# Clustered attention and two feed-forward layers on one core: a hand-placed order re-placed, with the first two pairs prepared in another order

## The chip, the cores and the metric

One core of a Trainium2 chip runs the whole program. The metric is device time in microseconds, median of three runs; the kernel before takes 791.06 us (790.3 to 793.32).

## The reference, cut to what matters

```python
def _attn_ref(q, k, v, centroids):            # q, k, v: 2 x 8 x 768 x 64, centroids: 8 x 16 x 64
    scale = 1.0 / np.sqrt(D)
    ...
    q_assign = np.argmax(np.einsum('bhsd,hcd->bhsc', q_n, c_n), axis=-1)
    k_assign = np.argmax(np.einsum('bhsd,hcd->bhsc', k_n, c_n), axis=-1)
    mask = q_assign[:, :, :, None] == k_assign[:, :, None, :]
    scores = np.where(mask, scale * q @ k.T, -1e9)
    attn = softmax(scores)
    return attn @ v

h = relu(x @ w_in) ** 2;      y = h @ w_out       # first layer, 1536 tokens, 512 -> 2048 -> 512
h = y @ w2_in;                out = (h * cos(h)) @ w2_out   # second layer
```

## The kernel before, in words

The 16 heads are worked two at a time, as eight **pairs**. For a pair, q and k are loaded (`load_raw`), turned on TensorE (`transpose_in`, L243), copied out by ScalarE in full (`full_copy`, L259), rounded to a high part (`high_part`, L252 and L254) and reduced to a low part (`low_part`, L265, on VectorE from PSUM). Products with the centroids (`sims`, L294), a transpose (`by_token`, L312), a maximum (`largest`, L319), its spreading and turning back (`spread`, `at_max`, L335), a comparison and a small product (`one_hot`, L348; `keep_one_hot`, L355) give one-hot rows of the nearest centroid. DMAs on SyncE's queue (SP) and ScalarE's put low parts, high parts and one-hot rows side by side (`stage`, `stage_own`, `stage_oh`), so that one product gives scores with the mask in it.

Each pair is 12 **units** of work of two kinds. `s_max` (L379; **M** below) computes scores with queries on partitions, and VectorE takes the row maxima (`s_largest`, L389). Six M give the maxima of half a pair's queries: `max_parts`, `max_cast` (L404), `max_rows` (L413), `max_keep` (L420) and the DMA `stage_max` (L427) bring them back as rows of the operand of the second kind. `scores` (L446; **S** below) computes scores with keys on partitions, ScalarE takes the exponential (L456), GpSimd adds the exponentials up (`add_up`, L468), and `pv` (L476) multiplies them with v. Then come the sums of a half pair (`sums`, L491), their inverse by way of DRAM, the division, and high and low parts of the output (`combine_low`, L555, on GpSimd). M, S, transposes and `max_rows` share three PSUM units; a unit is free again when VectorE or ScalarE has read it.

What sets the order is a table of numbers: every step has a time in units, `at(when, f, ...)` collects them, and they are emitted sorted by that time; each engine then runs its own instructions in that order, and SP its DMAs. Before the table comes a stretch written out by hand (L577 to L661) that prepares pair 0 and part of pair 1. `warm` issues small products of no use (L560): 20 at the start, and five times 8 between the first M (L1025).

Weights are loaded and split into two fp32r parts by VectorE in six operations per half chunk (L142 to L138), from the second half of pair 0 on. After attention `moe` runs 96 steps, each a product into the hidden layer (L697) and one out of it (L750) two steps later; `hooks` place the end of attention between the first of them. The last half pair's sums stand in step 1, ahead of the product of step 2.

```python
        if g + LEAD < NU:
            at(g + SMAX[c], s_max, g + LEAD)
            at(g + LARGEST[c], s_largest, g + LEAD)
    for when, _, f, a in sorted(steps_, key=lambda step: step[:2]):
        f(*a)
        1: [
            *(lambda u_=u_: pv(u_) for u_ in range(NU - GROUP, NU)), lambda: move_out(last + 1), lambda: sums(last + 1),
        ],
```

Of the kernel before, what the change touches and what calls it, by code (L numbers as in the profile page):

```python
# [25 lines left out]
LEAD = 9  # L26
# [4 lines left out]
WARM = 20  # L31
WARM_STEP = 8

FA = 8


@with_exitstack
def tile_kernel(ctx: ExitStack, tc: tile.TileContext, q, k, v, centroids, w1i, w1o, w2i, w2o, out):
# [177 lines left out]
    def load_heads(t, src, n, e=nc.sync):  # L216
        b, hp = pairs[n]
        e.dma_start(t, src[b, 2 * hp : 2 * hp + 2].rearrange("j (p t) d -> p t j d", t=NT))

    def load_raw(n, names, e=nc.sync):  # L220
        for nm in names:
            if nm == "v":
                t = ap.tile([P, NT, 2, D], F32, tag="rawv", name=f"rawv{n}", bufs=2)
            else:
                t = prepp.tile([P, NT, 2, D], F32, tag=f"raw{nm}", name=f"raw{nm}{n}")
            load_heads(t, {"q": q, "k": k, "v": v}[nm], n, e)
            raw[n, nm] = t
# [334 lines left out]

    cb = prepp.tile([P, NP, GC], F32, name="cb")
# [4 lines left out]
    load_raw(0, "q")  # L568
    load_raw(0, "k", nc.scalar)
    nc.scalar.activation(eps, half_t, AF.Exp)  # L570
    nc.gpsimd.memset(cb, 0.0)
    nc.vector.tensor_tensor(c2, cw, cw, ALU.mult)
# [3 lines left out]

    def constants(e, i):  # L577
        for j in range(2):
            e.memset(xq[i][R * (j + 1) : R * (j + 2)].bitcast(F32), 0.0)
            e.memset(xk[i][R * (j + 1) : R * (j + 2)].bitcast(F32), 0.0)  # L580

    def constants_own(e, i):
        for t in sets[i][:3]:
            for rows in OUTER:
                e.memset(t[rows, S:].bitcast(F32), -1.0 / R)

    def selection():
# [13 lines left out]
        nc.scalar.copy(first_of[:, : 2 * GC], firstf[:, : 2 * GC])  # L601
        nc.scalar.activation(first_of[:, 2 * GC :], firstf[:, 2 * GC :], AF.Copy, scale=-1.0)
# [6 lines left out]
        return first_of, oh_above, oh_scale  # L609
# [15 lines left out]
    transpose_in(0, "q")  # L625
    transpose_in(0, "k")
    full_copy(0, "q")
    full_copy(0, "k")
    load_raw(1, "qk")
    constants(nc.gpsimd, 0)  # L630
    first_of, oh_above, oh_scale = selection()
    constants_own(nc.gpsimd, 0)
    constants(nc.gpsimd, 1)
    for i in range(1, 3):
        constants_own(nc.gpsimd, i)
    high_part(0, "q", nc.vector)
    high_part(0, "k", nc.vector)
    stage(0, "k")
    stage_own(0)
    sims(0)  # L640
    keep_sims(0)
    by_token(0)
    largest(0)
    spread(0)
    low_part(0, "q")
    stage(0, "q")
    transpose_in(1, "q")
    at_max(0)
    compare(0)
    full_copy(1, "q")  # L650
    high_part(1, "q")
    one_hot(0)
    keep_one_hot(0)
    stage_oh(0, nc.scalar)
    low_part(0, "k")
    low_part(1, "q")
    transpose_in(1, "k")
    full_copy(1, "k")
    high_part(1, "k")
    low_part(1, "k")  # L660
    load_raw(0, "v")  # L661
# [196 lines left out]
    def moe(hooks):  # L858
# [38 lines left out]

    prep = [
        (-24.355, load_raw, "k"),
        (-22.864, load_raw, "q"),  # L900
        (-18.958, transpose_in, "k"),
        (-18.745, high_part, "k"),
        (-18.693, transpose_in, "q"),
        (-18.435, high_part, "q"),
        (-18.433, full_copy, "k"),
        (-18.030, low_part, "k"),
        (-17.583, full_copy, "q"),
        (-17.581, low_part, "q"),
        (-15.947, sims),
        (-15.367, keep_sims),  # L910
        (-13.090, by_token),
        (-12.080, largest),
        (-11.338, spread),
        (-9.239, at_max),
        (-9.222, compare),
        (-7.670, stage_own),
        (-7.153, one_hot),
        (-7.110, stage, "q"),
        (-6.620, keep_one_hot),
        (-4.098, stage, "k"),  # L920
        (-3.604, stage_oh),
    ]
    prep_second = [
        (-166.809, sims),
        (-141.396, keep_sims),
        (-140.871, by_token),
        (-123.691, largest),
        (-102.665, stage, "k"),
        (-94.621, spread),
        (-90.950, at_max),  # L930
        (-72.434, stage_own),
        (-39.797, stage, "q"),
        (-26.064, compare),
        (-10.377, one_hot),
        (-7.158, keep_one_hot),
        (-4.251, stage_oh),
    ]
    prep_all = [(4.558, load_raw, "v")]

    maxima = [  # L940
        (1.939, max_parts),
        (3.001, max_cast),
        (4.187, max_rows),
        (4.366, max_keep),
        (4.828, stage_max),
# [3 lines left out]
        (6.829, sums),  # L949
        (7.247, move_sums),  # L950
        (7.757, deal_sums),
        (9.940, invert),
        (9.986, move_out),
        (12.600, store_inverse),
        (13.702, load_inverse),
        (15.756, divide),
        (16.507, combine_high),
        (18.203, combine_low),
# [138 lines left out]
```

## Time and profile before

| | |
|---|---|
| median of three runs | 791.06 us |
| the profiled execution: its own time | 790.41 us |
| its span, first to last instruction | 788.4 us |
| TensorE (PE) busy | 765.1 us, 97% |
| VectorE (DVE) busy | 584.5 us, 74% |
| ScalarE (ACT) busy | 358.9 us, 46% |
| GpSimd (POOL) busy | 239.2 us, 30% |
| granted TensorE clock, mean | 0.994 |

Attention fills the first 262.8 us, the feed-forward layers the rest. A busy TensorE in this profile can still be one whose matmuls start late, since the ends are modelled; what a stage loses is read from its waits and from starts. Times in rows are microseconds from the start of the span.

### The profile page before, as it was taken

How to read it: one execution, taken by the hardware profiler on the slowest of the kernel's cores; microseconds unless marked ns; L12 is line 12 of the kernel's file. 1: busy time of each engine (PE TensorE's matmuls, PEld its weight loads, DVE VectorE, ACT ScalarE, POOL GpSimd, SP SyncE). 2: the span in 40 equal slices, each digit the busy share in tenths (PEclk: the TensorE clock that was granted, in tenths of full speed). 3: DMA queues.
4: the chain of work that ended last, by engine and by line, in shares of the span. 5: the costliest groups of instructions: out<-in, count | busy, mean ns of one | idle time of the engine just before them, and what ended most of it. 6: DMA issues, size and time to landing. Idle time of an engine off the chain costs nothing.

```text
span 788.4 us, 11444 instructions
## 1 busy us (share of the span) xinstructions
PE 765.1 (97%) x4293; PEld 586.1 (74%) x4293; DVE 584.5 (74%) x922; ACT 358.9 (46%) x609; POOL 239.2 (30%) x255
## 2 busy tenths in 40 slices
PE   6799999999999899999999999999999999999997
PEld 3575666666665688888888888888877788888886
DVE  4667787686789999969885216869999766676664
ACT  3265664665464445544444435353434433333332
POOL 7077797797999631000000000002222000000000
PEclk9899999999999999999999999999999999999999
DMA  4434545352335091037400005641000100010001
GB/s 121 121 94 117 135 102 137 79 122 57 110 95 186 7 373 58 0 107 242 158 29 1 0 1 166 206 128 35 0 1 1 54 1 1 0 54 1 0 1 54
DMA packets 76194, 62.19 MB, mean 79 GB/s; under 512 B 44896, under 2 KB 67436, under 8 KB 76140
## 3 DMA queue, kind: packets, MB, share of 16 engines
q1 hardware_dynamic: 74492, 60.99, 25.9%
q8 instruction: 33, 0.54, 0.3%
q10 hardware_dynamic: 1648, 0.49, 0.3%
q14 instruction: 21, 0.17, 0.1%
HBM read 48.27 MB, written 5.29 MB: 68 GB/s over the span
## 4 chain that ended last, share of the span: by engine, by line
PE 75%; DVE 16%; issue 3%; ACT 3%; POOL 1%; DMA 1%; ACTq 0%; SPq 0%; DVEq 0%; POOLq 0%
PE bank L750 27%; PE bank L697 13%; PE o_ps L697 13%; PE unit L446 7%; PE o_ps L476 5%; PE unit L379 4%; DVE ews L719 3%; DVE m L389 2%; DVE ews L718 2%; POOL acc L468 1%; DVE ews L730 1%; PE o_ps L294 1%; DVE aux L143 1%; DVE w L138 1%; DVE set L265 1%
## 5 line engine op out<-in xcount | busy, mean ns | idle before, releaser
L468 POOL TENSOR_TENSOR acc<-acc,p 128x384 f32<-128x384 f32 x128 | 139.9, 1128 | 2.8 <-ACT p L456 2.8
L750 PE MATMUL bank<-w,ewr 128*128 128x512 f32 x576 | 139.8, 391 | 0.4 <-DVE ewr L735 0.4
L750 PE MATMUL bank<-ewr,w 128*128 128x512 f32 x576 | 138.4, 389 | 0.0
L697 PE MATMUL bank<-xh,w 128*128 128x512 f32 x392 | 130.3, 394 | 0.0
L750 PEld LDWEIGHTS bank<-w,ewr 128*128 128x128 f32 x576 | 107.4, 188 | 25.4 <-POOL ewr L735 2.6
L750 PEld LDWEIGHTS bank<-ewr,w 128*128 128x128 f32 x576 | 108.1, 188 | 22.5
L735 POOL TENSOR_TENSOR ewr<-ews,ewr 128x512 fp32r<-128x512 f32 x24 | 32.8, 1365 | 302.9 <-ACT ewr L731 289.6
L389 DVE TENSOR_REDUCE m<-unit 128x2 f32<-128x768 f32 x96 | 88.8, 946 | 46.9 <-PE unit L379 42.0
L697 PE MATMUL o_ps<-xh,w 128*128 128x512 f32 x376 | 123.4, 389 | 0.0
L735 DVE TENSOR_TENSOR ewr<-ews,ewr 128x512 fp32r<-128x512 f32 x72 | 49.6, 689 | 54.9 <-ACT ewr L714 50.2
L697 PEld LDWEIGHTS bank<-xh,w 128*128 128x128 f32 x392 | 74.3, 190 | 17.1 <-issue 0.9
L697 PEld LDWEIGHTS o_ps<-xh,w 128*128 128x128 f32 x376 | 70.6, 188 | 14.7
L722 ACT ACTIVATE ews<-ews,narrow_t 128x512 f32<-128x512 f32 x48 | 34.9, 726 | 100.3 <-DVE ews L721 100.3
L456 ACT ACTIVATE p<-unit 128x768 f32<-128x768 f32 x96 | 71.0, 816 | 15.0 <-PE unit L446 13.2
L697 PE MATMUL bank<-xl,w 128*128 128x512 f32 x196 | 76.8, 392 | 0.0
L697 PE MATMUL o_ps<-xl,w 128*128 128x512 f32 x188 | 73.1, 389 | 0.0
L476 PE MATMUL o_ps<-p,rawv 128*64 128x384 f32 x384 | 69.0, 495 | 0.6 <-ACT x L527 0.6
L446 PE MATMUL unit<-set,set 64*128 64x384 f32 x512 | 65.1, 347 | 3.2 <-DVE set L265 2.0
L446 PEld LDWEIGHTS unit<-set,set 64*128 64x128 f32 x512 | 43.3, 184 | 15.3 <-issue 3.5
L137 ACT CAST w<-top 128x512 fp32r<-128x512 f32 x64 | 39.3, 616 | 32.1 <-DVE top L145 32.1
L138 DVE SCALAR_TENSOR_TENSOR w<-aux,aux 128x512 fp32r<-128x512 f32 x64 | 51.4, 803 | 1.7
L716 DVE TENSOR_SCALAR ews<-ews 128x512 f32<-128x512 f32 x48 | 20.3, 423 | 43.2 <-ACT ews L726 43.1
(122 smaller groups left out, 1074.8 us busy)
## 6 DMA issues: line engine op xcount, KB each, us to landing
wraw<-in_moe_w_in_dram SPq DMA_DIRECT2D x32, 512.0 KB
wraw<-in_moe_w_out_dram SPq DMA_DIRECT2D x32, 512.0 KB
rawq<-in_q_dram SPq DMA_DIRECT2D x8, 384.0 KB
ext<-set SPq DMA_DIRECT2D x32, 96.0 KB
rawv<-in_v_dram SPq DMA_DIRECT2D x8, 384.0 KB
rb<-row SPq DMA_DIRECT2D x32, 96.0 KB
rawk<-in_k_dram SPq DMA_DIRECT2D x7, 384.0 KB
held<-kept SPq DMA_DIRECT2D x8, 256.0 KB
```

Source lines behind the costliest of these rows:

```text
L137: nc.scalar.copy(w[:, 0], top.bitcast(F32))
L138: ve.scalar_tensor_tensor(w[:, 1], restf, 2.0**-20, power.bitcast(F32), ALU.mult, ALU.mult)
L379: nc.tensor.matmul(u[:, j, :HALF], lhsT=a[r, qs], rhs=b[r, ks], start=(p == 0), stop=(p == 1))
L389: nc.vector.tensor_reduce(d["m"][:, i, :, kh], u[:, :, :HALF], AX, ALU.max)
L446: nc.tensor.matmul(u[:, j, :HALF], lhsT=a[r], rhs=b[r, qs], start=(p == 0), stop=(p == len(ops) - 1))
L456: nc.scalar.activation(t, u[:, :, :HALF], AF.Exp, scale=SCALE)
L468: nc.gpsimd.tensor_tensor(accs[hb][:, j], a[:, j], ptiles[u_][:, j], ALU.add)
L476: nc.tensor.matmul(o_ps[0][j * D : (j + 1) * D, :HALF], lhsT=raw[n, "v"][:, kt, j, :], rhs=t[:, j], start=(kt == 0), stop=(kt == NT - 1),)
L697: nc.tensor.matmul(ph, lhsT=w[:, a, :], rhs=x[blk][:, a, :], start=(a == i == 0), stop=(a == KD - 1 and i == 2))
L722: nc.scalar.activation(e2, e2, AF.Sin, bias=hpi)
L735: e.tensor_tensor(al, e2, ah.bitcast(F32), ALU.subtract)
L750: nc.tensor.matmul(y, lhsT=a, rhs=b, start=(idx in opens and i == 0), stop=(idx in closes and i == 2))
```

## The change

Six edits. The hand-written stretch becomes a table (`prelude`) with the steps of pairs 0 and 1 in another order; pair 2 has a table of its own (`prep_third`), and so have the first 16 M (`SMAX_FIRST`). The low parts of pairs 0 to 2 are computed by GpSimd from the full copy in SBUF, not by VectorE from PSUM, and the PSUM unit is given back when the high part and the full copy are done. The first q and k are loaded head by head on two queues. The small products between the first M go, and there are 26 at the start for 20. All numbers of the steady tables are new; SHIFT is gone. The last half pair's sums stand one step later.

```diff
-WARM = 20
+WARM = 26
+FEW = 3
...
+        for j, e in enumerate(es or ()):
+            e.dma_start(t[:, :, j], src[b, 2 * hp + j].rearrange("(p t) d -> p t d", t=NT))
...
+        if n < FEW:
+            done_with(d, "t" + x)
...
-        nc.vector.tensor_tensor(
-            halves(d["l" + x]), wide(d["t" + x]), halves(d["h" + x].bitcast(F32)), ALU.subtract
-        )
+        high = d["h" + x].bitcast(F32)
+        if n < FEW:
+            nc.gpsimd.tensor_tensor(d["l" + x], d["f" + x], high, ALU.subtract)
+            return
+        nc.vector.tensor_tensor(halves(d["l" + x]), wide(d["t" + x]), halves(high), ALU.subtract)
...
-    load_raw(0, "q")
-    load_raw(0, "k", nc.scalar)
+    load_raw(0, "qk", (nc.sync, nc.scalar))
...
+    constants_own(nc.vector, 2)
+    for i in range(2):
         constants_own(nc.gpsimd, i)
...
+    prelude = [
+        (-308.5487, transpose_in, 0, "q"),
...
-        (4.828, stage_max),
+        (8.147, stage_max),
...
-    ADD, PV, WEIGHTS, WARMTH = 0.716, 1.525, 0.96, 0.97
+    ADD, PV, WEIGHTS, WARMTH = 1.481, -1.548, 0.96, 0.97
...
-    for g in range(-LEAD - 3, -7):
-        at(g + WARMTH, warm, WARM_STEP)
...
-            *(lambda u_=u_: pv(u_) for u_ in range(NU - GROUP, NU)), lambda: move_out(last + 1), lambda: sums(last + 1),
+            *(lambda u_=u_: pv(u_) for u_ in range(NU - GROUP, NU)), lambda: move_out(last + 1),
         ],
         2: [
-            lambda: move_sums(last + 1), lambda: invert(last + 1),
+            lambda: sums(last + 1), lambda: move_sums(last + 1), lambda: invert(last + 1),
```

TensorE before, from pair 1's `by_token` (L312) to the third M (the two lines of L379 are one M; `identb` is what `warm` multiplies):

```order
L312 MATMUL o_ps_66<-ident,sc_289 128x128 x3
L335 MATMUL o_ps_66<-ident,mxb_298 128x128 x3
L379 MATMUL unit_71<-set_1_106,set_0_105 128x384 x2
L379 MATMUL unit_71<-ext_1_118,ext_0_117 128x384 x2
L560 LDWEIGHTS identb
L560 MATMUL o_ps_65<-identb 128x128
```

and now, from the fifth M to the seventh (M is now L387, `at_max` L343, `max_rows` L421; `by_token` stands ahead of the first M as before):

```order
L387 MATMUL unit_72<-set_1_106,set_0_105 128x384 x2
L387 MATMUL unit_72<-ext_1_118,ext_0_117 128x384 x2
L387 MATMUL unit_70<-set_1_106,set_0_105 128x384 x2
L387 MATMUL unit_70<-ext_1_118,ext_0_117 128x384 x2
L343 MATMUL o_ps_66<-ident,mxb_301 128x128 x3
L421 MATMUL unit_71<-identr,set_3_108 64x128 x3
```

Six M now stand ahead of pair 1's `at_max`, with nothing between them, and `max_rows` follows at once; pair 1's `at_max` stood ahead of the first M.

GpSimd's queue now, from the last constants to the first low parts and the first sums (set_2 and set_3 are low parts of q and k; `fq`, `fk` the full copies):

```order
L578 MEMSET set_2_107 32x256 x2
L578 MEMSET set_0_109 32x256 x2
L578 MEMSET set_1_110 32x256 x2
L578 MEMSET set_2_111 32x256 x2
L273 TENSOR_TENSOR set_2_107<-fq_223,set_0_105 128x768
L273 TENSOR_TENSOR set_3_108<-fk_226,set_1_106 128x768
L573 MEMSET ext_0_119 32x768 x2
L573 MEMSET ext_1_120 32x768 x2
L273 TENSOR_TENSOR set_2_111<-fq_267,set_0_109 128x768
L273 TENSOR_TENSOR set_3_112<-fk_272,set_1_110 128x768
```

Pair 0's low part of q stands behind twelve constants; before, only memsets stood on this queue until the first sums.

TensorE at the end of attention before: the last two products of `pv` (L476), the last sums (L491) and the first rows of step 2's product (L697):

```order
L476 MATMUL o_ps_65<-p_3001,rawv_2758 64x384 x2
L476 MATMUL o_ps_65<-p_3045,rawv_2758 64x384 x2
L491 MATMUL o_ps_66<-acc_3030,ones 32x192 x4
L697 MATMUL bank_3087<-xh_90,w_2_0_1611 128x512
L697 MATMUL bank_3087<-xl_93,w_2_0_1611 128x512
```

and now, the last rows of step 2's product (L674), the last sums (L499) and the first of the product out of step 0 (L727):

```order
L674 MATMUL bank_3053<-xh_90,w_2_0_1584 128x512 x2
L674 MATMUL bank_3053<-xl_93,w_2_0_1584 128x512
L674 MATMUL bank_3053<-xh_90,w_2_0_1584 128x512
L499 MATMUL o_ps_66<-acc_3020,ones 32x192 x4
L727 MATMUL bank_3057<-ewr,w_0_1_1939 128x512 x3
```

The sums have moved behind the twelve matmuls of step 2.

## Rows read from the trace of the kernel before

**Rows 1.** The page, part 1: busy time and share of the span.

```profile
PE 765.1 (97%) x4293; PEld 586.1 (74%) x4293; DVE 584.5 (74%) x922; ACT 358.9 (46%) x609; POOL 239.2 (30%) x255
```

**Rows 2.** Windows: length, busy of PE, PEld, DVE, ACT, POOL; clock, DMA share, GB/s.

```profile
22.30:39.20 16.90, 13.88 (x107) 9.43 (x106) 12.30 (x16) 3.83 (x6) 0.00 (x0) 0.83 0.41 100
53.40:195.10 141.70, 140.06 (x1209) 91.13 (x1207) 107.46 (x144) 85.47 (x150) 116.03 (x114) 1.00 0.42 104
195.10:262.80 67.70, 62.89 (x504) 38.55 (x500) 56.58 (x64) 33.76 (x60) 63.67 (x58) 1.00 0.40 121
262.80:783.80 521.00, 520.62 (x2282) 428.32 (x2280) 387.82 (x666) 218.82 (x366) 35.26 (x27) 1.00 0.18 62
```

**Rows 3.** Chain that ended last, 0 to 64 us: start, length, piece.

```profile
23.35 0.97 PE o_ps L560 x8
...
25.89 1.82 PE o_ps L560 x16
...
28.38 0.55 PE o_ps L560 x8
```

**Rows 4.** Timeline, TensorE, 16 to 40 us: start, length, instruction, idle before it.

```profile
18.24 0.84 PE L294 MATMUL o_ps<-fk,cb 128*32 128x384 f32 x4 [1.42 <-ACT fk L259]
...
21.51 0.90 PE L335 MATMUL o_ps<-ident,mxb 128*128 128x128 f32 x3 [1.25 <-ACT mxb L326]
22.34 0.69 PE L379 MATMUL unit<-set,set 64*128 64x384 f32 x2
...
33.22 0.88 PE L243 MATMUL unit<-ident,rawk 128*128 128x128 f32 x6
...
39.17 0.61 PE L446 MATMUL unit<-set,set 64*128 64x384 f32 x4 [1.97 <-DVE set L265]
```

**Rows 5.** Timeline, ScalarE and its queue, 0 to 42 us.

```profile
15.87 1.42 ACTq L363 DMA_DIRECT2D ext<-ot  x2
...
32.42 0.48 ACT L420 CAST mr<-unit 64x384 fp32r<-64x384 f32 x1 [0.48 <-PE unit L413]
...
36.63 0.80 ACT L252 CAST set<-unit 128x768 fp32r<-128x768 f32 x1 [1.69 <-PE unit L243]
```

**Rows 6.** Timeline, all engines, 0 to 60 us: GpSimd's constants and three maxima.

```profile
8.98 2.10 POOL L585 MEMSET set<- 32x256 f32 x6
...
28.43 2.92 DVE L389 TENSOR_REDUCE m<-unit 128x2 f32<-128x768 f32 x3 [1.30 <-PE unit L379]
```

**Rows 7.** Timeline, SP, 30 to 60 us: the first maxima's two DMAs.

```profile
32.92 1.22 SPq L427 DMA_DIRECT2D set<-mr  x2
```

**Rows 8.** Chain, 140 to 150 us: a staging DMA from issue to landing.

```profile
144.02 1.97 DMA ext<-set
```

**Rows 9.** Timeline, GpSimd, 95 to 140 us: first sums of two half pairs a pair apart.

```profile
97.26 1.97 POOL L468 TENSOR_TENSOR acc<-p,p 128x384 f32<-128x384 f32 x2 [3.28 <-ACT p L456]
...
125.58 1.98 POOL L468 TENSOR_TENSOR acc<-p,p 128x384 f32<-128x384 f32 x2 [3.26 <-ACT p L456]
```

**Rows 10.** TensorE's waits, 40 to 220 us: total, times, longest.

```profile
PE unit L379 <- DVE set L265: 1.2, 5, 0.2
```

**Rows 11.** Timeline, TensorE, 117 to 127 us: three M in a row.

```profile
118.20 0.44 PE L379 MATMUL unit<-set,set 64*128 64x384 f32 x2
118.48 0.34 PE L379 MATMUL unit<-ext,ext 64*128 64x384 f32 x2
119.07 0.45 PE L379 MATMUL unit<-set,set 64*128 64x384 f32 x2 [0.25 <-DVE set L265]
```

**Rows 12.** Timeline, GpSimd, 196 to 266 us: the last sums, and the first step's low part.

```profile
248.61 1.33 POOL L555 TENSOR_TENSOR xl<-x,xh 128x384 fp32r<-128x384 f32 x1 [1.64 <-ACT xh L551]
...
262.24 1.73 POOL L735 TENSOR_TENSOR ewr<-ews,ewr 128x512 fp32r<-128x512 f32 x1
```

**Rows 13.** Timeline, TensorE, 256 to 271 us: last `pv`, last sums.

```profile
256.70 2.16 PE L476 MATMUL o_ps<-p,rawv 128*64 128x384 f32 x12
261.20 0.52 PE L491 MATMUL o_ps<-acc,ones 128*32 128x192 f32 x4 [2.34 <-POOL acc L468]
262.33 0.52 PE L491 MATMUL o_ps<-acc,ones 128*32 128x192 f32 x4 [0.62 <-POOL acc L468]
```

**Rows 14.** Chain, 205 to 275 us: step 2's product and the next one.

```profile
262.85 4.54 PE bank L697 x12
267.39 2.74 PE bank L750 x12
270.13 2.72 PE o_ps L697 x12
```

More of the change, by code (lines that the diff above doesn't have):

```diff
@@ L560, in warm, with constants, constants_own @@
             nc.tensor.matmul(o_ps[0][:, :P], lhsT=identb, rhs=identb, start=True, stop=True)
+    def constants(e, t):
+        for j in range(2):
+            e.memset(t[R * (j + 1) : R * (j + 2)].bitcast(F32), 0.0)
+    def constants_own(e, i):
+        for t in sets[i][:3]:
+            for rows in OUTER:
+                e.memset(t[rows, S:].bitcast(F32), -1.0 / R)
     cb = prepp.tile([P, NP, GC], F32, name="cb")
@@ L575, in tile_kernel @@
     nc.gpsimd.memset(eps, 1e-9)
[L577 to L585, printed above, removed]
     def selection():
@@ L624, in tile_kernel @@
         )
[L625 to L634, printed above, removed]
-        constants_own(nc.gpsimd, i)
[L636 to L661, printed above, removed]
+    constants(nc.gpsimd, xk[0])
+    firstf, first_of, oh_above, oh_scale = selection()
+    constants_own(nc.vector, 2)
+    for i in range(2):
+        constants_own(nc.gpsimd, i)
     LAG = 2
@@ new lines, in tile_kernel @@
+    prep = [
+        (-23.415, load_raw, "k"),
+        (-21.174, load_raw, "q"),
+        (-18.684, transpose_in, "q"),
+        (-18.509, high_part, "q"),
+        (-17.889, transpose_in, "k"),
+        (-17.719, full_copy, "q"),
+        (-16.865, high_part, "k"),
+        (-16.830, low_part, "q"),
+        (-16.797, full_copy, "k"),
+        (-15.546, sims),
+        (-15.239, keep_sims),
+        (-15.215, low_part, "k"),
+        (-12.577, by_token),
+        (-12.178, largest),
+        (-11.514, spread),
+        (-9.552, at_max),
+        (-9.348, compare),
+        (-7.211, stage_own),
+        (-6.804, one_hot),
+        (-6.049, keep_one_hot),
+        (-4.020, stage, "q"),
+        (-3.627, stage, "k"),
+        (-2.250, stage_oh),
@@ L922, in tile_kernel @@
     ]
     prep_second = [
[L924 to L936, printed above, removed]
-    ]
-    prep_all = [(4.558, load_raw, "v")]
-    maxima = [
[L941 to L944, printed above, removed]
-        (4.828, stage_max),
+        (-102.576, sims),
@@ new lines, in tile_kernel @@
+        (-90.698, keep_sims),
+        (-61.617, by_token),
+        (-42.144, largest),
+        (-32.182, spread),
+        (-27.559, stage, "k"),
+        (-21.941, at_max),
+        (-21.567, compare),
+        (-20.069, one_hot),
+        (-18.016, stage, "q"),
+        (-13.981, keep_one_hot),
+        (-2.669, stage_oh),
+        (5.831, stage_own),
+    ]
+    prep_all = [(6.723, load_raw, "v")]
+    prep_third = [
+        (-34.950, load_raw, "q"),
+        (-34.949, load_raw, "k"),
+        (-32.000, transpose_in, "k"),
+        (-31.980, full_copy, "k"),
+        (-31.960, high_part, "k"),
+        (-31.940, low_part, "k"),
+        (-31.920, transpose_in, "q"),
+        (-31.900, full_copy, "q"),
+        (-31.880, high_part, "q"),
+        (-31.860, low_part, "q"),
+        (-15.828, sims),
+        (-14.989, keep_sims),
+        (-13.022, by_token),
+        (-12.697, largest),
+        (-9.610, stage_own),
+        (-7.357, spread),
+        (-7.013, at_max),
+        (-6.970, compare),
+        (-6.339, one_hot),
+        (-5.173, stage, "q"),
+        (-4.787, stage, "k"),
+        (-4.179, keep_one_hot),
+        (-3.557, stage_oh),
+    ]
@@ L946, in tile_kernel @@
+    maxima_first = [
+        [(-18.700, max_parts), (-18.600, max_cast), (-18.400, max_rows), (-18.300, max_keep), (-18.200, stage_max)],
+        [(1.888, max_parts), (2.205, max_cast), (2.251, max_rows), (2.762, max_keep), (2.920, stage_max)],
+    ]
+    maxima = [
+        (4.201, max_parts),
+        (4.559, max_cast),
+        (5.436, max_rows),
+        (5.897, max_keep),
+        (8.147, stage_max),
     ]
     finish = [
-        (6.829, sums),
-        (7.247, move_sums),
-        (7.757, deal_sums),
@@ L952, in tile_kernel @@
[L952 to L958, printed above, removed]
+        (5.482, move_out),
+        (7.408, sums),
+        (7.869, move_sums),
+        (10.761, deal_sums),
+        (11.676, invert),
+        (13.168, store_inverse),
+        (14.298, load_inverse),
+        (16.259, divide),
+        (17.431, combine_high),
+        (18.530, combine_low),
```

124 lines of the change are left out of this document (76 added, 48 removed).

## The prediction

> **What bounds the kernel now.** First the page's busy times: TensorE works 97% of the span [rows 1], so only the other 3%, and time in which it does something useless or slow, can be won. Where that lies the table by stage tells: the feed-forward layers (262.8 to 783.8 us) leave TensorE 0.4 us idle in 521 [rows 2], and the change does not touch them beyond their first three steps. In the steady middle (53.4 to 195.1) TensorE is idle 1.6 us of 141.7. The first M stage (22.3 to 39.2) has 3.0 us idle of 16.9 and a granted clock of 0.83, and what fills part of its busy time are the small products, three of which stand in the chain that ended last [rows 3]. The end of attention (195.1 to 262.8) has 4.8 us idle of 67.7, and there GpSimd is busy 63.7 us [rows 2], so it is the bound. So three places have a price: the start, the waits too short for a table in the middle, and the hand-over.
>
> The sum is made against the profiled execution's own 790.41 us. The median of the runs shown is 0.65 us above it, and I add that at the end.
>
> **The start, up to the first S (at 39.17 [rows 4]).** I follow the new order piece by piece.
>
> The first M can run when pair 0's one-hot rows have landed: issued from 15.87 to 17.29 on ScalarE's queue [rows 5], and 1.97 us for such a transfer [rows 8], so about 19.3. In the trace it starts at 22.34, behind pair 1's `at_max`, which ends a string of waits; the product before it waited 1.42 us for a ScalarE copy [rows 4] that stood behind those two DMA issues. Now the copy is ahead of them and `at_max` behind six M. That is 3.1 us.
>
> What covers GpSimd's new low parts: pair 0's low part of q stands behind six constants more than the six that ended at 11.08 [rows 6], so it starts near 13.2. Its price is bounded by VectorE's rate (under 1 us, no gain on a path) and GpSimd's own two-operand adds, 1.97 us for two of half its size [rows 9]; I take the latter, the same engine and kind. It ends near 15.2, its two DMAs issue in about 1.2, as the maxima's two do [rows 7], and land 1.97 later: 18.4. So 0.9 us of cover before the one-hot rows' 19.3; past that every microsecond is lost on the first M. The loads split by head and the six more small products at the start I put at nothing: they lie beside each other ahead of the first transpose, and the one-hot chain behind it has its own dozen hand-overs. Bounds: 0.7 won, 0.7 lost.
>
> From the first M to the first maxima's DMA the trace takes 10.6 us (22.34 to 32.92 [rows 4, 7]). Without the small products VectorE is the limit: one M and its hand-over, some 1.0; six maxima of 0.97 (three in 2.92 [rows 6]); and from the last of them (31.35) to the DMA 1.6 as now. Together 8.4, so the DMA issues near 27.7, 5.2 earlier.
>
> Then the first S. The maxima land 1.22 + 1.97 later, at 30.9. But the last M ahead of it needs a PSUM unit that ScalarE empties in four copies of pair 2: k's transposes 0.3 after the DMA, as now (33.22 against 32.92 [rows 4, 7]), 0.88 long, then 4 x 0.80 [rows 5], then the M: 32.5. VectorE no longer has the low part that the trace waits 1.97 us for [rows 4]. So the first S comes near 32.5, 6.7 us earlier.
>
> The clock takes some of it back. In the trace it was granted at 0.83 on average in this stage [rows 2], although the small products filled gaps; without them I expect the half level (1.2 GHz) for longer. The M hide behind the maxima even so; the transposes of pair 2 (0.88 each) and what follows them do not. Bounds: 0 and 2.5 us (two transposes and pair 2's centroid products at half speed); I take 1.2. The Trainium skill says of this, in "TensorE: Matmul & The Clock Gate", Part 1, that "the default state is throttled, and activity releases the throttle", which speaks against taking the small products out; it is the second rival below. Start: **-5.5 us**, between -7.5 and -3.3 (the three pieces of the chain alone [rows 3]).
>
> **The steady middle.** A pair takes 28.3 us (97.26 to 125.58 [rows 9]). Named waits are small (the largest kind 1.2 us over 180 [rows 10]), but M start late by less: of two M in a row the second pair of matmuls starts 0.28 after the first, but the next M only 0.59 after that, 0.25 of it a named wait [rows 11]. I count some 1 us of such a pair that an order can win. In the new order M stand one or two at a time between S, sums and `pv`, so a unit has mostly been read when its turn comes. For five pairs at most -5. What it may cost is not shown by any row: `pv` and sums have other neighbours, and the maxima's DMA is issued later in a half block. I take half the gain: **-2.5 us**, between -5 and +2.
>
> **The hand-over.** TensorE ends its last `pv` at 258.86, waits 2.34 and 0.62 us for GpSimd's last sums [rows 13], then runs step 2's product in 4.54 where the same costs 2.72 at full clock [rows 14]. Now this product fills the wait. The product out of step 0 then starts not at 267.39 but when the sums are done (262.85) and GpSimd has the low part of step 0, at 262.24 + 1.73 = 264.0 [rows 12]: 3.4 us won. GpSimd's sums do not come earlier for it, so TensorE still idles before them, and the 1.8 us of half clock may fall on the next product: 1.6 to 3.4, I take 2.5. GpSimd's own wait of 1.64 [rows 12] may shrink: 0.5. Together **-3 us**, between -1.5 and -5. VectorE's weight splitting stands in the same order; the layers after it have TensorE full [rows 2], so what is won before stays won.
>
> Sum: 790.4 - 5.5 - 2.5 - 3 = 779.4, and with 0.65 for the median **780.0 us**.
>
> **Rivals.** (a) *Everything at its better end*: start -7.5, middle -5, hand-over -5, so 773.6. For it: the chain of waits in the first 40 us is loose almost everywhere. Against: GpSimd is busy 94% of the last attention stage, and any gain of TensorE there ends at it.
>
> (b) *The clock stays low into the first S.* Without the small products TensorE works in short pieces between maxima from 19 to 28 us. If the half level lasts until the first half block is through, the start's 5.5 us are gone: 785.5. For it: the clock of 0.83 despite the small products [rows 2]. Against: by 28 us the M and two transposes stand close together.
>
> (c) *The start's gain is given back at the low parts.* GpSimd has six of them at about 2 us ahead of its first sums. If its queue runs 5 us later than I reckon, the 0.9 us of cover is gone, the first M waits for the low part's staging and the first sums start late: 4 of the 5.5 us and 4 more by the hand-over are lost, since GpSimd bounds the end: near 788.
>
> (d) *Slower: the maxima land too late.* `stage_max` now stands behind the loads of inverses and the sums' DMA on SP, 8.147 against 4.828 units. S needs it in each half block. By the new order `max_rows` comes some 7 us into a half block of 13 to 14; with 0.48 for its copy [rows 5], 1.22 and 1.97 for its DMA it lands near 11, some 2.4 us in time. Should SP reach it over 2.4 us later than that (a wait for a landing ahead of it on the queue), each half block of pairs 1 to 7 stalls; 1.5 us beyond that point, 14 times, is +21, so 801. For it: SP runs in order, and two waits for landings stand ahead of this DMA. Against: the queue has idle stretches, and the loads ahead depend on work one half block older.
>
> **How the numbers follow.** A measurement of this kernel can tell about 0.5% from no change, 4 us, so faster is below 787.1 and slower above 795.0. Forecast 0.60; (a) 0.13; (b) 0.12; (c) 0.08; (d) 0.07. Faster: the first three, with a little of (c), 0.87; same: the rest of (c), 0.07; slower: most of (d), 0.06. The forecast's own range is 776 to 784. To hold eight in ten the range takes in most of (a) and (b): 772.5 to 787.5.
>
> **What would show it.** Right: first M near 19 to 20 us, first S near 32 to 34, a pair in 27.5 to 28 us, step 2's product ending ahead of the last sums, hidden layers as before. The start is wrong if the first S comes after 36; the middle if a pair takes 28.3 or more; the hand-over if the product out of step 0 starts more than 4 us after the last sums. The whole is wrong if S wait for `stage_max` or if GpSimd's first low part ends after 17 us.

## The result, and the profile after

The changed kernel takes 778.4 us, median of four runs (777.18 to 779.09), against 791.51 for four of the kernel before: ratio 0.983, 95% interval 0.981 to 0.985. It is faster by 1.7%, and 1.6 us below the forecast of 780.0. Five more runs (`after_again` below) gave 777.27 us (776.65 to 777.73), ratio 0.9825 (0.981 to 0.984). The profiled run is the slowest of the first four, 779.09 us with a span of 777.4, 11.0 less than the 788.4 of before.

The page of the changed kernel, part 1, against [rows 1]:

```profile
PE 757.2 (97%) x4259; PEld 585.6 (75%) x4259; DVE 582.6 (75%) x922; ACT 360.6 (46%) x609; POOL 248.2 (32%) x255
```

TensorE lost 7.9 us of busy time, the 40 small products taken out and some 1.1 us in each steady pair among it; its half clock was longer than before (granted clock 0.988 on average for 0.994). GpSimd gained 9. For where the time went I use two marks that every run has: the first addition that GpSimd makes of a half block's exponentials, and the start of the last 48 matmuls in the chain that ended last. What remains behind these matmuls takes 3.8 to 4.6 us in the profiles, and 7.0 in one (`sums_only`), so totals of single runs differ by more than the marks. First the kernel before (timeline of GpSimd: half blocks 0, 11 and 15; last row of the chain):

```profile
42.18 1.99 POOL L468 TENSOR_TENSOR acc<-p,p 128x384 f32<-128x384 f32 x2 [24.03 <-ACT p L456]
...
195.11 1.99 POOL L468 TENSOR_TENSOR acc<-p,p 128x384 f32<-128x384 f32 x2 [0.91 <-ACT p L456]
...
249.90 2.16 POOL L468 TENSOR_TENSOR acc<-p,p 128x384 f32<-128x384 f32 x2
...
772.93 10.89 PE bank L750 x48
```

The same views of the changed kernel, with two rows more for the length of a pair:

```profile
36.81 1.99 POOL L476 TENSOR_TENSOR acc<-p,p 128x384 f32<-128x384 f32 x2 [0.80 <-ACT p L464]
...
90.26 1.98 POOL L476 TENSOR_TENSOR acc<-p,p 128x384 f32<-128x384 f32 x2 [2.10 <-ACT p L464]
...
117.19 1.98 POOL L476 TENSOR_TENSOR acc<-p,p 128x384 f32<-128x384 f32 x2 [2.10 <-ACT p L464]
...
183.71 1.98 POOL L476 TENSOR_TENSOR acc<-p,p 128x384 f32<-128x384 f32 x2 [0.32 <-ACT p L464]
...
240.27 2.16 POOL L476 TENSOR_TENSOR acc<-p,p 128x384 f32<-128x384 f32 x2
...
762.31 10.89 PE bank L727 x48
```

And of a second profile of the same kernel (`after_again` below):

```profile
34.88 1.98 POOL L476 TENSOR_TENSOR acc<-p,p 128x384 f32<-128x384 f32 x2 [0.84 <-ACT p L464]
...
181.74 1.99 POOL L476 TENSOR_TENSOR acc<-p,p 128x384 f32<-128x384 f32 x2 [0.34 <-ACT p L464]
...
238.24 2.16 POOL L476 TENSOR_TENSOR acc<-p,p 128x384 f32<-128x384 f32 x2
...
760.22 10.89 PE bank L727 x48
```

The differences of these rows make the ledger of the whole study:

| stretch | before | after | after, again | won | forecast |
|---|---|---|---|---|---|
| to the first addition | 42.18 | 36.81 | 34.88 | 5.4 / 7.3 | 5.5 |
| from there to half block 11 | 152.93 | 146.90 | 146.86 | 6.0 / 6.1 | 2.5 |
| half blocks 11 to 15 (the last two pairs) | 54.79 | 56.56 | 56.50 | -1.8 / -1.7 | 0 |
| from half block 15 to the last 48 matmuls | 523.03 | 522.04 | 521.98 | 1.0 / 1.1 | 3 |
| sum | 772.93 | 762.31 | 760.22 | 10.6 / 12.7 | 11 |

The sum of 11 came near (by the medians timed side by side the gain is 13.1), but of its terms only the start did: the middle gave more than twice the forecast, the last two pairs gave a part of it back, and the hand-over gave a third of what I expected.

**The start.** Timeline of TensorE in the changed kernel, 14 to 35 us:

```profile
14.49 0.84 PE L302 MATMUL o_ps<-fq,cb 128*32 128x384 f32 x4 [1.89 <-ACT fq L265]
16.26 1.49 PE L302 MATMUL o_ps<-fk,cb 128*32 128x384 f32 x4 [0.93 <-ACT fk L265]
...
19.21 0.69 PE L387 MATMUL unit<-set,set 64*128 64x384 f32 x2
...
29.23 1.49 PE L247 MATMUL unit<-ident,rawk 128*128 128x128 f32 x6
...
34.30 0.51 PE L454 MATMUL unit<-set,set 64*128 64x384 f32 x4
```

First M at 19.21 where 19.3 was forecast, first S at 34.30 where 32.5 was (39.17 before [rows 4]). But the M does not wait for the one-hot rows. It stands behind pair 1's centroid products, which wait for ScalarE's full copies, and those wait for something new (timelines of ScalarE and of GpSimd):

```profile
13.64 0.80 ACT L265 COPY fq<-unit 128x768 f32<-128x768 f32 x1 [2.60 <-POOL set L273]
```

```profile
7.66 4.07 POOL L578 MEMSET set<- 32x256 f32 x12
11.80 1.81 POOL L273 TENSOR_TENSOR set<-fq,set 128x768 fp32r<-128x768 f32 x1
```

The low part on GpSimd reads the full copy of pair 0, there is one buffer for it, and pair 1's copy must wait until it is read: 2.60 us. The chain that ended last runs the same way: GpSimd's twelve constants, its two low parts (3.58 us together), ScalarE's copy of k, the centroid products, the first M. Putting the constants behind the low parts was not tried. The second difference to the forecast is the clock. Windows of the changed kernel (PEclk is the granted clock; 0.50 is 1.2 GHz, 1.00 is 2.4 GHz):

```profile
15.27:22.09 6.82, 5.26 (x25) 2.97 (x23) 2.36 (x4) 2.49 (x4) 6.55 (x7) 0.50 0.34 89
...
25.51:32.33 6.82, 6.12 (x30) 5.15 (x32) 3.96 (x7) 2.35 (x5) 0.00 (x0) 0.50 0.43 101
```

Twice 6.82 us at half clock stand ahead of the first S here. In the second profile of the same kernel the same work has one such stretch of about 3 us:

```profile
15.00:25.50 10.50, 6.00 (x43) 3.29 (x43) 6.43 (x9) 3.24 (x7) 6.87 (x7) 1.00 0.60 146
26.00:28.50 2.50, 2.50 (x15) 1.98 (x12) 2.50 (x4) 0.00 (x0) 0.00 (x0) 0.50 0.29 73
```

Its first M comes at 18.18 and its first S at 32.34, 0.2 from the forecast. Both profiles start pair 1's products with q at the same time (14.49 and 14.46), and behind them the same operations are longer at half clock (the products with k 1.49 us for 0.84, the second set of pair 2's transposes 1.49 for 1.03). So the 2.0 us between the two profiles are the clock's.

**The last two pairs.** TensorE's waits in the changed kernel, 183.7 to 240.3 us (4.2 us; before, 195.1 to 249.9, they were 1.8):

```profile
PE unit L454 <- DVE m L397: 1.7, 2, 1.3
PE bank L674 <- ACT p L464: 1.2, 1, 1.2
PE unit L454 <- DMA set<-mr: 1.1, 1, 1.1
```

The third is rival (d)'s mechanism, maxima that land too late. It occurs once, in the last half block, and not in the pairs before: from 60 to 190 us the view lists no wait of TensorE at all.

**The hand-over.** GpSimd and TensorE in the changed kernel, against [rows 12] and [rows 13]:

```profile
239.29 1.02 POOL L563 TENSOR_TENSOR xl<-x,xh 128x384 fp32r<-128x384 f32 x1 [3.09 <-ACT xh L559]
...
242.39 10.31 POOL L476 TENSOR_TENSOR acc<-acc,p 128x384 f32<-128x384 f32 x8
252.66 1.72 POOL L712 TENSOR_TENSOR ewr<-ews,ewr 128x512 fp32r<-128x512 f32 x1
```

```profile
251.61 0.52 PE L499 MATMUL o_ps<-acc,ones 128*32 128x192 f32 x4 [0.30 <-POOL acc L476]
252.75 0.52 PE L499 MATMUL o_ps<-acc,ones 128*32 128x192 f32 x4 [0.62 <-POOL acc L476]
253.20 0.49 PE L727 MATMUL bank<-ewr,w 128*128 128x512 f32 x1
254.43 4.27 PE L727 MATMUL bank<-ewr,w 128*128 128x512 f32 x11 [0.74 <-POOL ewr L712]
```

Step 2's product fills the wait as forecast (2.34 became 0.30), GpSimd's own wait has not shrunk but grown, from 1.64 to 3.09, and the half clock fell on the next product (4.27 for eleven matmuls). No cost of that half clock shows at the end: in the second profile the same eleven take 2.79 us, step 2's product then waits 0.98 us for GpSimd, and the last stretch is as long (521.98 for 522.04):

```profile
252.40 2.79 PE L727 MATMUL bank<-ewr,w 128*128 128x512 f32 x11 [0.73 <-POOL ewr L712]
...
264.75 2.81 PE L727 MATMUL bank<-ewr,w 128*128 128x512 f32 x11 [0.98 <-POOL ewr L712]
```

### The profile page after: what moved, and what is told of

Its sections match the earlier page's. It is cut to its first block, busy times and chain, and to the rows that moved or that the text cites. A ratio compares the mean times of both kernels' runs of the same rounds, so it can differ in the third digit from the quotient of the medians.

```text
span 777.4 us, 11394 instructions
## 1 busy us (share of the span) xinstructions
PE 757.2 (97%) x4259; PEld 585.6 (75%) x4259; DVE 582.6 (75%) x922; ACT 360.6 (46%) x609; POOL 248.2 (32%) x255
## 4 chain that ended last, share of the span: by engine, by line
PE 77%; DVE 15%; POOL 3%; issue 3%; ACT 2%; DMA 0%; POOLq 0%; DVEq 0%; ACTq 0%
PE bank L727 28%; PE o_ps L674 13%; PE bank L674 13%; PE unit L454 8%; PE o_ps L484 6%; PE unit L387 5%; DVE ews L696 3%; DVE ews L695 2%; DVE m L397 1%; PE unit L247 1%; POOL acc L476 1%; DVE top L146 1%; DVE ews L707 1%; DVE aux L144 1%; DVE top L145 1%
## 5 line engine op out<-in xcount | busy, mean ns | idle before, releaser
L476 POOL TENSOR_TENSOR acc<-acc,p 128x384 f32<-128x384 f32 x128 | 141.8, 1139 | 4.6 <-ACT p L464 4.5
L727 PE MATMUL bank<-ewr,w 128*128 128x512 f32 x576 | 140.6, 393 | 0.8 <-POOL ewr L712 0.7
L727 PE MATMUL bank<-w,ewr 128*128 128x512 f32 x576 | 139.7, 391 | 0.7 <-DVE ewr L712 0.7
L674 PE MATMUL bank<-xh,w 128*128 128x512 f32 x392 | 129.0, 390 | 1.2 <-ACT p L464 1.2
L727 PEld LDWEIGHTS bank<-ewr,w 128*128 128x128 f32 x576 | 108.9, 190 | 24.8 <-POOL ewr L712 1.3
L727 PEld LDWEIGHTS bank<-w,ewr 128*128 128x128 f32 x576 | 107.4, 188 | 25.7 <-POOL ewr L712 2.4
L674 PE MATMUL o_ps<-xh,w 128*128 128x512 f32 x376 | 123.4, 389 | 0.0
L674 PEld LDWEIGHTS bank<-xh,w 128*128 128x128 f32 x392 | 73.6, 188 | 18.0 <-ACT p L464 1.5
L674 PEld LDWEIGHTS o_ps<-xh,w 128*128 128x128 f32 x376 | 70.5, 188 | 14.7
L674 PE MATMUL bank<-xl,w 128*128 128x512 f32 x196 | 76.3, 389 | 0.0
L674 PE MATMUL o_ps<-xl,w 128*128 128x512 f32 x188 | 73.1, 389 | 0.0
L454 PEld LDWEIGHTS unit<-set,set 64*128 64x128 f32 x512 | 45.9, 184 | 7.0 <-DVE m L397 3.6
```

Of the source, the lines that this page charges most:

```text
L454: nc.tensor.matmul(u[:, j, :HALF], lhsT=a[r], rhs=b[r, qs], start=(p == 0), stop=(p == len(ops) - 1))
L476: nc.gpsimd.tensor_tensor(accs[hb][:, j], a[:, j], ptiles[u_][:, j], ALU.add)
L674: nc.tensor.matmul(ph, lhsT=w[:, a, :], rhs=x[blk][:, a, :], start=(a == i == 0), stop=(a == KD - 1 and i == 2))
L727: nc.tensor.matmul(y, lhsT=a, rhs=b, start=(idx in opens and i == 0), stop=(idx in closes and i == 2))
```

## The experiments

Every kernel was timed beside the kernel before, and its ratio is to that. `after_again` is the changed kernel unedited; it ran on one chip with `xl_late`, `f_two` and `low_dve`. `sums_only`, `sums_back`, `mid_only` and `mid_sums` had another chip, and `old_head`, `warm_hold`, `tail_late` and `best` a third, where a comparison with `after_again` by medians goes across chips; the kernel before had medians of 790.97, 790.43 and 790.97 us on the three.

> The changed kernel unedited, as the measure for the edits run beside it: 777 to 779 us. If the place of the half clock at the start varies from run to run, its profile shows the first S anywhere from 32.3 to 34.3 us, with the span following it.

Measured: 777.27 us, ratio 0.9825 (0.981 to 0.984). First S at 32.34, as said above; edits of the changed kernel are compared with this.

**What the hand-over is worth.** `sums_only`, the kernel before with the last edit of the change alone:

```diff
-            *(... pv ...), lambda: move_out(last + 1), lambda: sums(last + 1),
+            *(... pv ...), lambda: move_out(last + 1),
         ],
         2: [
-            lambda: move_sums(last + 1), ...
+            lambda: sums(last + 1), lambda: move_sums(last + 1), ...
```

> The kernel before with one edit: the last half block's sums go behind step 2's output product. Theory (the hand-over is a term of its own, worth what the trace after suggests): the product that was held behind the sums runs while GpSimd still adds, so the end comes 2 to 3 us earlier, 788.5 to 789.5 us. Rival (GpSimd's additions set the end anyway, and the product only fills a wait that then opens elsewhere): 791 to 792 us, no change.

Measured: 789.82 against 790.43 us, 0.6 us by the medians; ratio 0.9986 (0.9977 to 0.9995), so 1.1 us (0.4 to 1.8): between the two. The profile shows why. Counted from the start of half block 15's additions (250.44 and 249.90), step 1's y product comes 3.3 us earlier (269.96 in place of 272.69), as the forecast's 3.4 had it. But waits appear that the kernel before does not have (TensorE's waits from 258 us on):

```profile
PE bank L750 <- POOL ewr L735: 1.7, 2, 1.0
```

The smaller of the two (0.73) is at step 0; the larger (0.97) is that of step 2's y product for GpSimd's low part of step 2, at 276.96, and behind it the gain is 1.8 us, counted the same way (step 3's y product at 282.30 in place of 283.57). `sums_back` is the same edit undone in the changed kernel.

> The changed kernel with that one edit undone: the last sums ahead of step 2's product again. Theory: 2 to 3 us are lost, 780.5 to 781.5 us. Rival (in the changed kernel GpSimd is later against TensorE than before, so more or less depends on the sums): if the wait for GpSimd's additions is fully exposed, over 3 us lost, 782 us or more; if the product is hidden anyway, 778.4.

Measured: 779.47 us, ratio 0.9856 (0.984 to 0.987). With `after_again` at 0.9825 that is 2.4 us lost, as the theory had it, with some 1.5 of uncertainty. Its profile has its first additions and its half block 15 where `after_again` has them (34.82 and 238.22), and its last 48 matmuls at 762.68 against 760.22. So the edit is worth about 2.5 us behind the new tables and 1.1 behind the old ones; the ledger's 1.0 is less than 2.5 because the new tables end worse (in `sums_back` half block 15 to the last matmuls takes 524.46 us, before 523.03). The next two runs, which have the new tables behind the old start, say the same: 523.96 us without the edit and 521.43 with it.

**What the middle is worth.** `mid_only` is the kernel before up to pair 2 with the new steady tables (`prep_o`, `SCORES_o` and so on) from pair 3 on (`K0 = 3`); `mid_sums` has the last sums moved too.

```diff
-        for r, f, *a in prep if n > 1 else prep_second:
+        for r, f, *a in (prep_o if K0 <= n < K1 else prep) if n > 1 else prep_second:
...
+            o = K0 <= g // SP < K1
-            at(g + SCORES[c], scores, g)
+            at(g + (SCORES_o if o else SCORES)[c], scores, g)
```

> The kernel before up to pair 2, and the changed kernel's steady tables from pair 3 on (one half block between them has its value products at a time in between); old start, old last sums. Theory (the tables save 1.4 us in every pair that is placed by them, some five, less what GpSimd gives back at the end): 784 to 786 us. Rival (the forecast's size of half a microsecond a pair): 788.5 to 789.5 us. Second rival (the shorter pair comes from the new start, which leaves other pairs ahead): 791 us.

> As the last, with the last sums moved as well: all of the change but its start. Theory (start worth 4 to 5.5 us): 782.5 to 784 us, so that the difference to the changed kernel's 778.4 is the start. Rival (the start's gain is eaten by the longer half clock and GpSimd's low parts, and the middle carries nearly all): 779 to 780 us.

Measured: 797.05 us (ratio 1.009, 1.008 to 1.010) and 794.59 us (1.005, 1.004 to 1.006): both slower than before, and all the expectations missed. The totals say nothing of the tables, since the joint between two tables costs more than they win. What tells is the length of a pair behind the joint (GpSimd's first additions in `mid_sums`, half blocks 4, 6, 8 and 10):

```profile
99.21 1.98 POOL L468 TENSOR_TENSOR acc<-p,p 128x384 f32<-128x384 f32 x2 [4.08 <-ACT p L456]
...
127.88 1.98 POOL L468 TENSOR_TENSOR acc<-p,p 128x384 f32<-128x384 f32 x2 [3.31 <-ACT p L456]
...
160.33 1.98 POOL L468 TENSOR_TENSOR acc<-p,p 128x384 f32<-128x384 f32 x2 [2.85 <-ACT p L456]
...
187.26 1.98 POOL L468 TENSOR_TENSOR acc<-p,p 128x384 f32<-128x384 f32 x2 [2.11 <-ACT p L456]
```

Old tables 28.67, the joint 32.45, new tables 26.93, with the old start ahead of them. The changed kernel has 26.93 (90.26 to 117.19), the kernel before 28.32 [rows 9]. So the 1.4 us a pair belong to the tables and not to the new start, which was the second rival. The start's worth can't be read from `mid_sums`, because of the joint.

**What the start is made of.** `low_dve` puts the low parts of the first three pairs back on VectorE (`FEW = 0` for `FEW = 3`); with that a PSUM unit is given back only behind the low part again.

> The changed kernel with the low parts of its first three pairs on VectorE, read from PSUM as before, everything else in place. Theory A (the 1.8 us that each takes on GpSimd holds ScalarE and SP's queue, VectorE does it in 0.95): 1 to 2 us faster, 776.5 to 777.5 us. Theory B (the forecast's: VectorE's maxima are what the first pairs wait for, and two to six low parts of 0.95 us would stand in front of them): 1 to 3 us slower, 779.5 to 781.5 us.

Measured: 778.89 us, ratio 0.9846 (0.983 to 0.986), 1.6 us slower than `after_again`, at intervals that overlap. Both theories have their part in it. ScalarE's wait is gone and the first M comes at 16.92, 1.3 us earlier; but then VectorE is late with pair 2 (timeline of TensorE, 30 to 35 us):

```profile
31.18 0.44 PE L387 MATMUL unit<-set,set 64*128 64x384 f32 x2 [1.43 <-DVE set L275]
...
33.26 0.52 PE L302 MATMUL o_ps<-fq,cb 128*32 128x384 f32 x2 [1.46 <-DVE ot L363]
```

First S at 34.50, 2.2 us later. By these waits GpSimd's low parts are worth it for pair 2 and cost time for pair 0. `f_two` takes that cost away: pair 0's full copies lie in two probability buffers that are not used yet.

```diff
-        d["f" + x] = prepp.tile([P, S], F32, tag="f" + x, ...)
+        if n:
+            d["f" + x] = prepp.tile([P, S], F32, tag="f" + x, ...)
+        else:
+            i = 9 + "qk".index(x)
+            d["f" + x] = ap.tile([P, 2, HALF], F32, tag=f"p{i}", ...).rearrange("p j c -> p (j c)")
```

> The changed kernel with the full copies of pair 0 in two probability buffers that are idle then, so that pair 1's copies don't wait for GpSimd's low parts (2.60 and 0.27 us on ScalarE, 1.89 on TensorE in the profile). Theory (that wait is on the path to the first M, rival c of the forecast in part): first M and first S 1 to 2 us earlier, 776.5 to 777.5 us. Rival (the first M waits next for the one-hot rows, issued late behind SP's and ScalarE's queues): under 0.5 us, 778 us.

Measured: 776.41 us, ratio 0.9814 (0.980 to 0.983), 0.9 us faster than `after_again`, though the intervals overlap. The first M comes at 16.34 (18.18) and now does meet the one-hot rows, for only 0.43 us:

```profile
17.21 0.78 PE L391 MATMUL unit<-ext,ext 64*128 64x384 f32 x2 [0.43 <-DMA ext<-ot]
```

Of the 1.8 us at the first M 0.8 reach the first S (31.55) and the end. The other 1.0 is lost within the first M: by this wait, and by the half clock that this run has from 17 to 27 us (0.78 for these two matmuls, 0.33 in `after_again`).

`old_head` undoes the split loads (one DMA for q, one for k) and the six more small products (`WARM = 20`).

> The changed kernel with pair 0's loads whole again (q by SP, k by ScalarE) and 20 small products ahead instead of 26. Theory (the forecast's: worth nothing, 0.7 us either way): 776.6 to 778 us. Rival (the trace after: first transposes nearly a microsecond earlier and 0.82 us instead of 1.54 us for six, so the one-hot chain 2 us earlier): first M 0.5 to 1.5 us later, 778 to 779 us.

Measured: 778.21 us, ratio 0.9840 (0.9825 to 0.9856), 0.9 us slower and in the rival's range; the intervals overlap. The first transposes start at 6.32, waiting 0.84 for the whole of q, in place of 5.18, and the first additions come 0.7 later (35.54). But the first M comes only 0.16 later (18.34), short of the rival's 0.5; the rest arises behind it, where this run has half clock from 23.7 to 30.5 us and `after_again` from 25.6 to 29.0. So the profile shows no more than 0.16 us for the edit, inside the forecast's 0.7 either way; whether the longer half clock belongs to the edit is not shown. Nor do the six more small products decide how fast the first transposes run: with 26 of them six take 0.82 us in `after_again` and 1.49 in `f_two`.

`warm_hold` puts 48 small products into TensorE's waits of the first 25 us.

```diff
+    prelude += [(-200.0, warm, 6), (-167.0, warm, 8), (-129.4, warm, 12), (-60.0, warm, 6), (-18.45, warm, 16)]
```

> The changed kernel with 48 more small products between the operations of the first two pairs, in places where TensorE waits (6, 8, 12 and 6 in the first pair's and the second pair's chain, 16 ahead of the first maximum's rows). Theory (the half clock between 15 and 32 us costs up to 2 us, and fuller stretches keep the clock up): no half level before the first S in the granted clock, first S at 31 to 32.3 us, 775.5 to 776.8 us. Rival (the products stand in front of TensorE's own work, or the level falls all the same): first S later than 32.3 us, 777.3 to 778.5 us.

Measured: 776.57 us (776.4 to 777.0), ratio 0.9820 (0.9805 to 0.9836), 0.7 us faster by the medians and 0.4 by the ratios, within the intervals. The window of the start:

```profile
8.00:34.00 26.00, 20.93 (x187) 13.80 (x185) 16.45 (x23) 11.07 (x20) 17.13 (x21) 1.00 0.57 135
```

The half level is gone from the granted clock, in all four runs (1.00 over the span, where the changed kernel's nine runs have 0.988 to 0.998). Its record leaves something out, though: the first six transposes, at 5.27, take 1.49 us, as at half clock, where it shows 1.00. First M at 18.73, 0.5 later than in `after_again`, first S at 31.83, 0.5 earlier. The Trainium skill's sentence that the forecast quoted from "TensorE: Matmul & The Clock Gate", Part 1, agrees with this run. So against a profile with a short half stretch the 48 products give 0.5 us at the first S, against the first profile 2.5.

**What holds the end.** `xl_late` moves the low part that made GpSimd wait 3.09 us.

```diff
     finish_last = finish_late[:4]
+    finish_late = finish_late[:-1]
...
-            lambda: divide(last), lambda: combine(last), load_mid,
+            lambda: combine_low(last - 1), lambda: divide(last), lambda: combine(last), load_mid,
```

> The changed kernel with the low part of half block 13 (the one that made GpSimd wait 3.09 us for ScalarE's copy, ahead of the last half block's additions) issued at step 2, behind those additions. Theory (GpSimd's row of additions sets the last sums, and through the next low part the first y product): the additions end 3 to 4 us earlier, the sums stand right behind step 2's product, the y product of step 0 starts 1.5 to 2.5 us earlier; 776 to 777 us. Rival (the additions then wait for the last exponentials instead): less than 0.5 us gained, 778 us.

Measured: 776.50 us, ratio 0.9816 (0.980 to 0.983), 0.8 us under `after_again`, within the intervals. GpSimd did what the theory says: the additions of half block 15 start at 233.94 in place of 238.24, and step 0's y product at 249.44, 1.7 us earlier. But the last 48 matmuls start at 760.18, as in `after_again`, so a gain at the end is not shown. Step 2's y product gives the time back: it waits 0.94 for ScalarE and 0.99 for GpSimd, and its last eleven matmuls, of which part ran at half clock, take 4.07 us for 2.81. They start 1.2 us earlier than in `after_again`, and the half clock takes just that; what the edit is worth at full clock is open. The two waits have one source, and `after_again` shows it on ScalarE:

```profile
260.79 0.61 ACT L559 CAST xh<-x 128x256 fp32r<-128x256 f32 x2 [3.11 <-DVE x L538]
261.31 0.59 ACT L689 ACTIVATE ews<-bank 128x512 f32<-128x512 f32 x1
```

Step 2's first elementwise operation (L689) stands behind the high parts of half block 14, for which ScalarE waits 3.11 us until VectorE has divided; in `xl_late` it is 4.79. The product that it reads has long been done. GpSimd's low part of step 2 stands behind half block 14's too, but waits 0.28 us more for ScalarE. `tail_late` moves the division and both parts of half block 14.

```diff
-            lambda: combine_low(last - 1), lambda: divide(last), lambda: combine(last), load_mid,
+            load_mid,
         ],
+        3: [lambda: combine_low(last - 1), lambda: divide(last), lambda: combine(last)],
```

> The changed kernel with the low part of half block 13 and the division and both parts of half block 14 issued at step 3, so that GpSimd's additions of half block 15 and its low part of step 2 stand behind neither. Theory (the hand-over's gain and that of the earlier additions are lost again at step 2's y product, which waits 0.9 to 1.9 us for GpSimd's low part, queued behind half block 14's): y product of step 0 2 us earlier, no wait at that of step 2, 775 to 776 us. Rival (VectorE's weight splits, 97% busy from 245 to 270 us, hold the elementwise work of the first steps anyway): the wait is back at steps 2 or 3, 776.3 to 777.3 us.

Measured: 775.12 us, ratio 0.9800 (0.978 to 0.982), 2.1 us under `after_again` by the medians and 2.0 by the ratios, whose intervals just overlap. From the first additions (35.56) to the last 48 matmuls (758.89) are 723.33 us; the changed kernel has 725.50 and 725.34. A wait of 1.0 us remains at steps 3 and 4:

```profile
PE bank L727 <- POOL ewr L712: 1.0, 2, 0.6
```

That VectorE holds this stage, as the rival has it, shows in `after_again` in the chain that ended last, which runs through its splits of the weights (rows from 249 to 257 us):

```profile
249.85 1.38 DVE top L146
...
256.02 0.70 DVE top L146
```

`best` joins `tail_late` and `f_two`.

> tail_late with pair 0's full copies in the two idle probability buffers as well. Theory (start and end add up): 0.7 to 1 us less than tail_late, 774.3 to 775.2 us. Rival (what the start gains is taken at the hand-over by GpSimd or VectorE): as tail_late.

Measured: 773.22 us (three runs at 773.07 to 773.26, one at 775.74), ratio 0.9784 (0.9765 to 0.9804): 4.1 us under `after_again` by the medians, 3.2 by the ratios, and the fastest of the study. The profiled run is the one of 775.74, with near 10 us at half clock ahead of its first S (33.51); its first M (18.43) is no earlier than that of `tail_late` (18.21), and from first additions to last matmuls it takes 723.29 us, as `tail_late`. That `f_two`'s gain adds to the end's is so shown by the medians alone (1.9 us under `tail_late`). Small products in TensorE's waits on top of `best` were not tried.

What these starts win reaches the end: from the first addition to the last 48 matmuls `after_again`, `f_two`, `old_head` and `warm_hold` take 725.34, 725.40, 725.61 and 725.40 us, whenever they begin. Only `low_dve`, which begins 2.2 us later, takes 724.57 and so has 0.8 of it back.

## Why the prediction was right, and where it was not

That the total came out is in part luck: in the first profile the 3.5 us that the middle gave above its term stand against 1.8 and 2.0 that the last two pairs and the hand-over fell short.

**The start, -5.5: right in size, by another path.** First M at 19.21 for 19.3, the maxima's DMA issued at 27.32 for 27.7; the half clock put 1.0 us on that first M, and without it the second profile has 18.18 and 25.71, so the agreement at these two points is luck. And the step "the first M can run when pair 0's one-hot rows have landed" named the wrong wait. They would have been there, by a little (the last of their DMAs was issued at 16.1 and landed 2.2 later, and with the other wait gone `f_two` meets them); the M waited for pair 1's centroid products, held by GpSimd's low part through the one buffer of the full copy. I had costed that low part only by what it delays behind itself (its staging), and not by what it keeps from being overwritten. Rival (c) had the right actor and another mechanism. The price of the low part, near 2 us, was 1.81; it ended at 13.61, not 15.2, so the cover that I worried about was wide.

**The clock, 1.2 of 0 to 2.5: inside, but not one number.** The same program shows its first S at 32.34 and at 34.30. Rival (b), the half level up to the first S, is what the first profile shows; it costs 2 us more than the second, not 5.5, because the M hide behind the maxima, as the prediction said.

**The middle, -2.5: too small, -6.0.** The step that failed is "I take half the gain". The 1 us that I counted in a pair was too little and all of the 1.4 was won. TensorE has 0.25 us of idle time in the pair from 97.26 to 125.58 of the kernel before and none in one of the changed kernel, with 245 matmuls in both (windows, first before and then after; the first two numbers behind the times are the length and TensorE's busy time):

```profile
97.26:125.58 28.32, 28.07 (x245) 18.22 (x243) 21.79 (x29) 17.13 (x31) 23.47 (x23) 1.00 0.45 115
```

```profile
90.26:117.19 26.93, 26.93 (x245) 18.39 (x243) 21.78 (x29) 17.38 (x31) 23.53 (x23) 1.00 0.47 120
```

So most of the gain lies in pauses too short for the view of waits, which the modelled ends count as busy. Which of the table's rows closes them was not tried.

**The last two pairs, 0: +1.8.** No term stood for them. What the pairs win comes to an end in which VectorE is busier: its busy time between half blocks 11 and 15 went from 43.9 to 47.1 us (54 instructions, now 56), and TensorE waits for it there. `sums_only` took 55.63 us for this stretch, with the old tables and nothing moved ahead of its end, so the loss lies between 0.9 and 1.8; `mid_sums`, new tables behind the old start, has 55.84. What in the tables or the start causes it stays open.

**The hand-over, -3: too large, -1.1 to -2.5 for the edit, -1.0 in the ledger.** The 3.4 us at the first y products are there in `sums_only` (3.3). What failed is "what is won before stays won": two steps further on the elementwise work of step 2 is late, queued on ScalarE behind half block 14's high parts, which wait for a division that stands among VectorE's splits. And GpSimd's wait did not shrink; it grew to 3.09. "So it is the bound" was half the truth too: `xl_late` shows that GpSimd does not bound the end alone. With its additions 4.3 us earlier the end is the same, in a profile where the half clock took the last 1.2 of them; with half block 14's division out of the way as well (`tail_late`) 2.0 us reach the end.

**Rival (d)** did not decide: one wait of 1.1 us, in the last half block.

## What to carry to other kernels

A step moved to an idle engine reads its inputs later and longer: ask which buffer it keeps from being written again, not only who waits for its result. A wait that is filled at a seam between two stages was paid out here only when the waits behind it had slack as well; follow the chain to where the bound engine is full again before booking the gain. And where a table of times is exchanged, compare the length of a steady period: totals of mixed tables are spoiled by the joint.

## What the hardware showed that was not expected

The granted clock at the start is not a property of the program: the same kernel had twice 6.82 us at the half level in one profile and about 3 us in another, 2 us apart at the first S, and with 48 small products in TensorE's waits it was recorded at the full level in every run.

VectorE's splits slow down beside GpSimd's additions. Groups of VectorE in `after_again`, from 238.3 to 250.6 us, where GpSimd adds without a pause:

```profile
L146 DVE SCALAR_TENSOR_TENSOR top<-wraw,top 128x512 uint32<-128x512 uint32 x2 | 2.8, 1378 | 0.1
L145 DVE TENSOR_SCALAR top<-wraw 128x512 uint32<-128x512 uint32 x2 | 2.5, 1226 | 0.0
```

and from 300 to 500 us, where GpSimd is idle:

```profile
L146 DVE SCALAR_TENSOR_TENSOR top<-wraw,top 128x512 uint32<-128x512 uint32 x32 | 22.2, 692 | 1.0
L145 DVE TENSOR_SCALAR top<-wraw 128x512 uint32<-128x512 uint32 x32 | 13.5, 421 | 0.0
```

1.38 us against 0.69, and 1.23 against 0.42. The chain shown with `tail_late` has the same within one stage: `top` (L146) takes 1.38 us at 249.85, beside GpSimd's additions, and 0.70 at 256.02, where GpSimd is idle. The Trainium skill, "GPSIMD Engine Reference", Specifications, says that the two engines share their interfaces to SBUF and names this contention for instructions of VectorE with two SBUF inputs or in a two-port mode; the rows agree, without showing which of the two holds for the one-input operation. This would make VectorE and GpSimd hold the end of attention together, and work moved between the two win less than its duration there; no run tests that by itself.
